# Loading v by batch and selecting the global values on chip in a two-layer attention kernel

## The chip, the cores and the metric

The kernel runs on one core of a Trainium2 chip. The metric is the device time of a run in microseconds (us). A profile of one execution gives the span from the first to the last instruction, which is a little shorter than the device time. The core has a matrix engine (TensorE, PE in the profile; its weight loads are PEld), VectorE (DVE), ScalarE (ACT), GpSimd (POOL), and SyncE (SP), which only issues transfers (DMA) here. Each engine works through its own instructions in order and waits for others by semaphores.

## The reference

Two layers are computed for 4 batches of 768 positions. The first is an attention with 8 heads of 64, in which a query sees the first 8 keys ("global") and the 96 keys up to itself ("local"), with a bias that falls with the distance. Its output is the input of the second, a mixture of 4 causal attention experts of width 64, of which each position takes its best two.

```python
# layer 1: q, k, v are [4, 8, 768, 64]
scores = q @ k.T / 8
is_global = pos_k < 8
is_local  = (0 <= pos_q - pos_k) & (pos_q - pos_k < 96)
dist  = where(is_global & ~is_local, 96, abs(pos_q - pos_k))
scores = where(is_global | is_local, scores - slope[h] * dist, -1e9)
x = softmax(scores) @ v            # -> [4, 768, 512]
# layer 2
logits = x @ w_gate                # weights w of the best two of 4 experts
for e in range(4):
    ye = softmax(causal((x @ wq[e]) @ (x @ wk[e]).T / 8)) @ (x @ wv[e]) @ wo[e]
    out += w[e] * ye               # where e is among the two
# ... cut
```

## The kernel before

The work is cut into 24 units u of 128 positions, six per batch. For each unit there are stages: loads of k, q and v (`lk`, `lq`, `lv`), casts to 16 bits on GpSimd (`kc`, `qc`, `vc`), transposes of k and q (`tk`, `tq`), local scores in two halves (`sa`, `sb`) with their exponentials on ScalarE, global scores (`gs`, one for three units), global and local values (`vg`, `va`, `vb`), the transpose of the result (`tx`), and then the second layer (`pk`, `pq`, `pv` projections, `ro` routing, `ca` to `cc` causal scores, `ma` mask, `za`, `zb` values, `tz` transpose, `ou` output). A fixed string ORDER lists all stages one after the other, and each engine executes its instructions in that order.

```python
dma = nc.sync.dma_start            # SyncE's queue; S_ is ScalarE, V VectorE, G GpSimd
# NT = 6 units per batch, NH = 3, HG = 4, KB = 64, W = 159, WP = 320, VW = 65
# ... constants, on VectorE, before everything else: cut
for hh in range(2):
    r = slice(hh * KB, hh * KB + KB)
    for p in range(NP):                                   # L81: 8 instructions
        V.scalar_tensor_tensor(biasT[r, p, :], rel[r, :], -slopes[2 * p + hh] / sc1,
                               lt[r, :], op0=Alu.mult, op1=Alu.add)
# ... cut
psS = fast.enter_context(tc.tile_pool(name="psS", bufs=2, space=PSUM))   # score buffers
# ... cut
def load_v(i):                     # i counts 4 per group of 3 units: v comes by half batch
    g, hq = divmod(i, HG)
    b, r0 = divmod(g * NH, NT)
    issue = S_.dma_start if g == 0 else dma
    if hq == 0:
        fs["v", g] = raw.tile([P, HG, 2 * NH, Dh], F32, name="vf", bufs=3)
        if r0 == 0:
            for p in range(NP):                           # L232: the 8 global rows of v
                issue(vgbuf[b % 2][32 * p:32 * p + 2 * NG, 0:Dh],
                      v[b, 2 * p:2 * p + 2, 0:NG, :])
    for hf in range(2):                                   # L235: 64 partitions, 96 KB
        issue(fs["v", g][hf * KB:(hf + 1) * KB, hq, :, :],
              v[b, hf * HG + hq, r0 * P:(r0 + NH) * P, :].rearrange("(c j) d -> j c d", j=KB))

def cast(u, nm):
    if nm != "v":
        # ... cut: q and k, L243, G.tensor_copy to 16 bits
        return
    v16, first = take("vbuf", u)
    if first:
        G.memset(v16[:, :, :, Dh:VW], 1.0)                # L247: a column of ones
    r = u % NH                                            # L249
    G.tensor_copy(v16[:, :, :, 0:Dh], fs["v", u // NH][:, :, 2 * r:2 * r + 2, :]
                  .rearrange("r h c d -> r c h d"))

def globals_in(b):                 # GpSimd: global keys, and global values with a mask
    # ... cut: kg
    G.tensor_tensor(vg[:, :, :], vgbuf[b % 2][:, :].unsqueeze(1).to_broadcast([P, H, VW]),
                    vmask[...], op=Alu.mult)              # L278, mask cut

def local_scores(u, g):
    if u not in as_:
        as_[u], first = take("abuf", u)
        if first:                                         # 5 buffers, zeroed on first use
            G.memset(as_[u][:, :, :, 0:KB], 0.0)          # L312
            G.memset(as_[u][:, :, :, KB + W:WP], 0.0)     # L313
    # ... cut: matmuls L319 (bias), L326 (scores); exponential L329 into abuf

def local_values(u, i):            # L356: 32 matmuls of 64x65 per unit (16 in a batch's first)
    # ... cut
    # then reciprocal of the sums (L363) and product (L365) on VectorE
```

Of the kernel before, what the change touches and what calls it, by code (L numbers as in the profile page):

```python
# [19 lines left out]
P = 128  # L20
# [3 lines left out]
def kernel(  # L24
# [23 lines left out]
    WP = KB + W + P - (W - P)  # L48
# [17 lines left out]
    with tc.tile_pool(name="setup", bufs=1) as setup:  # L66
        rel_i = setup.tile([P, W], I32)
        G.iota(rel_i[:, :], pattern=[[1, W]], channel_multiplier=-1, base=0)
        rel = setup.tile([P, W], F32)
        V.tensor_copy(rel[0:KB, :], rel_i[0:KB, :])  # L70
        V.tensor_scalar(rel[KB:P, :], rel_i[KB:P, :], float(KB), None, op0=Alu.add)
        ge = setup.tile([P, W], F32)
        V.tensor_scalar(ge[:, :], rel[:, :], 0.0, None, op0=Alu.is_ge)
        lt = setup.tile([P, W], F32)
        V.scalar_tensor_tensor(lt[:, :], rel[:, :], float(NL), ge[:, :],
                               op0=Alu.is_lt, op1=Alu.mult)
        V.tensor_scalar(lt[:, :], lt[:, :], -1.0, -NEG, op0=Alu.add, op1=Alu.mult)
        for hh in range(2):
            r = slice(hh * KB, hh * KB + KB)
            for p in range(NP):  # L80
                V.scalar_tensor_tensor(biasT[r, p, :], rel[r, :], -slopes[2 * p + hh] / sc1,  # L81
                                       lt[r, :], op0=Alu.mult, op1=Alu.add)
            V.tensor_copy(ident2[r, :], ident[r, r])


    row_i = const.tile([P, 1], I32)
    G.iota(row_i[:, :], pattern=[[0, 1]], channel_multiplier=1, base=0)
    key_i = const.tile([P, 1], I32)
    V.tensor_scalar(key_i[:, :], row_i[:, :], NG - 1, None, op0=Alu.bitwise_and)
    key_f = const.tile([P, 1], F32)  # L90
    V.tensor_copy(key_f[:, :], key_i[:, :])
    col_i = const.tile([P, P], I32)
    G.iota(col_i[:, :], pattern=[[1, P]], channel_multiplier=0, base=0)
    col_f = const.tile([P, P], F32)
    V.tensor_copy(col_f[:, :], col_i[:, :])
    grel = const.tile([P, P], F32)
    V.tensor_scalar(grel[:, :], col_f[:, :], key_f[:, :], None, op0=Alu.subtract)
    g_lo = const.tile([P, P], F32)
    V.tensor_scalar(g_lo[:, :], grel[:, :], 0.0, NEG, op0=Alu.is_ge, op1=Alu.mult)
    g_hi = const.tile([P, P], F32)  # L100
    V.tensor_scalar(g_hi[:, :], grel[:, :], float(NL), None, op0=Alu.is_lt)
    gmask = const.tile([P, P], F16)
    V.tensor_mul(gmask[:, :], g_lo[:, :], g_hi[:, :])
    gbias = const.tile([P, 1], F32)
    for p in range(NP):
        V.memset(gbias[32 * p:32 * p + 32, :], -slopes[2 * p] * NL)
    odd_i = const.tile([P, 1], I32)
    V.tensor_scalar(odd_i[:, :], row_i[:, :], NG, None, op0=Alu.bitwise_and)
    odd = const.tile([P, 1], F32)
    V.tensor_copy(odd[:, :], odd_i[:, :])  # L110
    V.tensor_scalar(odd[:, :], odd[:, :],
                    (slopes[1] / slopes[0] - 1.0) / NG, 1.0,
                    op0=Alu.mult, op1=Alu.add)
    V.tensor_mul(gbias[:, :], gbias[:, :], odd[:, :])


    vmask = const.tile([P, NP, 2], F32)
    G.memset(vmask[:, :, :], 1.0)
    G.affine_select(out=vmask[:, :, :], in_=vmask[:, :, :], pattern=[[-32, NP], [-NG, 2]],
                    channel_multiplier=1, base=0, compare_op=Alu.is_ge, fill=0.0)  # L120
    G.affine_select(out=vmask[:, :, :], in_=vmask[:, :, :], pattern=[[32, NP], [NG, 2]],
                    channel_multiplier=-1, base=NG - 1, compare_op=Alu.is_ge, fill=0.0)
    kmask = const.tile([P, 32], F16)
    V.memset(kmask[:, :], 0.0)
    V.memset(kmask[0:Dh, 0:NG], 1.0)
    V.memset(kmask[Dh:P, NG:2 * NG], 1.0)
# [62 lines left out]
    def ring(name, n, shape):  # L189
        rings[name] = [big.tile(shape, F16, name=f"{name}{i}") for i in range(n)], {}  # L190

    def take(name, u):

        bufs, owner = rings[name]
        first = u % len(bufs) not in owner
        owner[u % len(bufs)] = u
        return bufs[u % len(bufs)], first

    def held(name, u):
        bufs, owner = rings[name]  # L200
        assert owner[u % len(bufs)] == u
        return bufs[u % len(bufs)]

    ring("abuf", NA, [P, 2, HG, WP])
    ring("vbuf", NV, [P, 2, HG, VW])
    ring("v2buf", NV2, [P, E, VW])
    vgbuf = [big.tile([P, VW], F32, name=f"vgbuf{i}") for i in range(2)]
    for t in vgbuf:
        G.memset(t[:, 0:Dh], 0.0)
        G.memset(t[:, Dh:VW], 1.0)  # L210


    fs, kqT, gl, ags, xTs, kqs, lgs, wts, a2s, as_, done = ({} for _ in range(11))
    s16s, zs_, x16s, routing, zss, zts, tps, ppss, zs2 = ({} for _ in range(9))

    def load(u, nm):
        b, ri = divmod(u, NT)
        f = fs[nm, u] = raw.tile([P, H, Dh], F32, name=nm + "f")
        dma(f[:, :, :], {"k": k, "q": q}[nm][b, :, ri * P:(ri + 1) * P, :]  # L219
            .rearrange("h j d -> j h d"))  # L220

    def load_v(i):


        g, hq = divmod(i, HG)
# [592 lines left out]
```

## Time and profile before

| | |
|---|---|
| device time, three runs | 169.4, 169.53, 171.94 us; median 169.53 |
| the profiled run | 169.96 us, span 168.1 us, mean granted TensorE clock 0.978 |
| chain that ended last, by engine | PE 45%, DMA 19%, SyncE's queue 17%, POOL 4%, DVE 4% |
| transfers | 27.88 MB, mean 166 GB/s, pieces of 256 bytes nearly throughout |
| the two transfer queues' share of 16 engines | 64.5% and 2.1% |
| loads of k and q | 24 each of 256 KB |
| loads of v | 56 on SyncE's queue and 8 on ScalarE's, of 96 KB each |
| loads of the global rows of v | 12 and 4, of 4 KB each |

Busy time counts the instructions of an engine that run, with overlapping ones counted once. A wait is idle time of an engine in front of an instruction, put down to what ended it: "A <- B" reads "A waited for B". The chain that ended last is followed back from the last instruction to whatever released it, step by step. "L356" is line 356 of the kernel. In the timeline a row gives the start, the length, the engine, the line, the operation, output <- input and the count of instructions, and in brackets the idle time before it with what ended it.

### The profile page before, as it was taken

The page shows a single profiled execution, that of the slowest core. Times are in us where ns is not written, and L with a number is a line of the kernel's source. Part 1 is how long each engine was busy: PE and PEld are TensorE (multiplying, and loading weights), DVE is VectorE, ACT ScalarE, POOL GpSimd, SP SyncE. Part 2 cuts the span into 40 slices and gives each one's busy share as a digit, 9 for nine tenths or more (in the row PEclk, how much of TensorE's full clock was granted, in tenths as well). Part 3 has the DMA queues.
Part 4 walks back from the last instruction along what each step waited for, and adds up shares of the span by engine and source line. Part 5 has one row for each costly group of instructions (what it writes and reads, how often), then busy time and mean ns, then how long its engine had stood idle before and what let it go on. Part 6 is the DMA issues. An engine that isn't in the chain of part 4 may idle for free.

```text
span 168.1 us, 6984 instructions
## 1 busy us (share of the span) xinstructions
PE 135.2 (80%) x2918; PEld 104.1 (62%) x2918; DVE 108.2 (64%) x338; ACT 91.7 (55%) x137; POOL 90.7 (54%) x246
## 2 busy tenths in 40 slices
PE   0446499979999779959999789929999999999710
PEld 0234277958867559738778569717776788776400
DVE  7631246468887748747877578715787786887520
ACT  0007227472966537755756764516769867589420
POOL 4550999994956086618666496158632253533100
PEclk9999999999999999999999999996999999999995
DMA  5999975994897697479985837896246112031550
GB/s 127 258 273 287 241 141 131 228 210 107 187 207 169 157 274 176 99 165 293 243 196 116 221 90 180 212 233 159 96 115 188 66 66 102 28 131 64 193 194 12
DMA packets 86296, 27.88 MB, mean 166 GB/s; under 512 B 82928, under 2 KB 82928, under 8 KB 86256
## 3 DMA queue, kind: packets, MB, share of 16 engines
q1 hardware_dynamic: 82984, 26.54, 64.5%
q10 hardware_dynamic: 3272, 0.80, 2.1%
q8 instruction: 25, 0.41, 1.0%
q14 instruction: 15, 0.12, 0.2%
HBM read 21.05 MB, written 6.29 MB: 163 GB/s over the span
## 4 chain that ended last, share of the span: by engine, by line
PE 45%; DMA 19%; SPq 17%; POOL 4%; DVE 4%; issue 3%; ACT 3%; POOLq 0%; ACTq 0%; DVEq 0%
PE pps L386 8%; SPq L235 8%; DMA vf<-in_v_dram 8%; DMA qf<-in_q_dram 6%; PE cps L434 5%; PE zps L356 5%; PE vps L400 5%; PE zps L462 4%; SPq L219 4%; PE ops L490 4%; SPq L232 4%; PE tp L257 4%; PE sps L319 3%; DMA kf<-in_k_dram 3%; PE xps L371 2%
## 5 line engine op out<-in xcount | busy, mean ns | idle before, releaser
L437 ACT ACTIVATE a<-cps 128x1024 f16<-128x1024 f32 (+1 forms) x48 | 42.2, 917 | 16.2 <-PE cps L434 16.0
L329 ACT ACTIVATE abuf<-sps 128x636 f16<-128x636 f32 (+1 forms) x48 | 30.8, 683 | 24.3 <-PE sps L326 24.0
L249 POOL CAST vbuf<-vf 128x512 f16<-128x512 f32 x24 | 14.4, 616 | 25.9 <-DMA vf<-in_v_dram 19.7
L356 PE MATMUL zps<-vbuf,abuf 64*128 64x65 f16 x704 | 15.9, 193 | 10.7 <-POOL vbuf L249 9.3
L266 DVE COPY kqT<-tp 128x1024 f16<-128x1024 f16 x24 | 16.4, 690 | 9.4 <-PE tp L257 9.2
L356 PEld LDWEIGHTS <-abuf 64*128 64x128 f16 x704 | 14.6, 96 | 12.6 <-issue 10.5
L449 POOL TENSOR_SCALAR_AFFINE_SELECT a<-a 128x256 f16<-128x256 f16 x48 | 18.3, 409 | 5.7 <-ACT a L437 5.4
L391 DVE CAST kq<-pps 128x512 f16<-128x512 f32 x24 | 16.5, 690 | 6.2 <-PE pps L386 5.9
L243 POOL CAST s16q<-qf 128x512 f16<-128x512 f32 x24 | 14.7, 613 | 10.5 <-DMA qf<-in_q_dram 10.4
L363 DVE RECIPROCAL rinv<-zps 128x8 f32<-128x8 f32 x24 | 5.0, 206 | 20.1 <-PE zps L356 20.0
L493 ACT ACTIVATE osb<-ops 128x512 f32<-128x512 f32 x24 | 14.1, 598 | 6.6 <-PE ops L490 2.1
L365 DVE TENSOR_TENSOR x<-zps,rinv 128x512 f16<-128x512 f32 x24 | 16.6, 691 | 0.8
L257 PE MATMUL tp<-ident,s16k 128*128 128x128 f16 x96 | 10.8, 243 | 7.4 <-POOL s16k L243 7.4
L243 POOL CAST s16k<-kf 128x512 f16<-128x512 f32 x24 | 14.8, 617 | 3.0 <-DMA kf<-in_k_dram 2.4
L319 PE MATMUL sps<-biasT,ident 64*64 64x318 f16 (+1 forms) x192 | 15.1, 319 | 0.9 <-ACT ag L300 0.9
L462 PE MATMUL zps<-v2buf,a 128*128 128x65 f16 x336 | 15.3, 194 | 0.2
L386 PE MATMUL pps<-xT,wq 128*128 128x128 f16 x192 | 14.6, 219 | 0.0
L386 PE MATMUL pps<-xT,wk 128*128 128x128 f16 x192 | 14.6, 219 | 0.0
L326 PE MATMUL sps<-kqT 64*64 64x159 f16 (+2 forms) x384 | 14.5, 232 | 0.0
L490 PE MATMUL ops<-wo,zt 128*128 128x512 f16 x48 | 14.1, 390 | 0.4 <-DVE zt L483 0.4
L400 PE MATMUL vps<-wvg,xT 128*128 128x260 f16 x96 | 14.1, 275 | 0.1
L462 PEld LDWEIGHTS <-a 128*128 128x128 f16 x336 | 13.2, 98 | 1.5 <-DVE zs L473 0.6
(98 smaller groups left out, 257.2 us busy)
## 6 DMA issues: line engine op xcount, KB each, us to landing
kf<-in_k_dram SPq DMA_DIRECT2D x24, 256.0 KB, 3.8
qf<-in_q_dram SPq DMA_DIRECT2D x24, 256.0 KB, 4.9
out_dram<-osb SPq DMA_DIRECT2D x24, 256.0 KB, 2.8
vf<-in_v_dram SPq DMA_DIRECT2D x56, 96.0 KB, 3.0
vf<-in_v_dram ACTq DMA_DIRECT2D x8, 96.0 KB, 4.3
w<-in_moe_wk_dram SPq DMA_DIRECT2D x1, 512.0 KB
w<-in_moe_wq_dram SPq DMA_DIRECT2D x1, 512.0 KB
w<-in_moe_wv_dram SPq DMA_DIRECT2D x1, 512.0 KB, 4.5
```

Source lines behind the costliest of these rows:

```text
L243: G.tensor_copy(s16s[nm, u][:, :, :], f[:, :, :])
L257: nc.tensor.transpose(tps[u][:, i, p, :], s16s["kq"[i], u][:, 2 * p:2 * p + 2, :].rearrange("j h d -> j (h d)"), ident[:, :])
L319: mm(s_ps[o, hh, 0:2 * w].rearrange("r (c n) -> r c n", c=2), lhsT=ident2[r, :], rhs=biasT[r, p, 0:w].unsqueeze(1).to_broadcast([KB, 2, w] ...
L329: S_.activation(as_[u][:, :, 2 * g:2 * g + 2, KB:KB + w], s_ps[:, :, 0:2 * w].rearrange("r h (c n) -> r h c n", c=2), func=Exp, scale=sc1)
L356: mm(zs_[u][:, hf, hq * VW:(hq + 1) * VW], lhsT=held("abuf", u - prev)[r, hq % 2, hq // 2 * 2 + c, at:at + P], rhs=held("vbuf", u - prev)[ ...
L365: V.tensor_tensor(x16s[u][:, :, :, :], z4[:, :, :, 0:Dh], rinv.unsqueeze(3).to_broadcast([P, 2, HG, Dh]), op=Alu.mult)
L386: mm(p_ps[:, i, ep, :], lhsT=w[:, ko, ep, :, :].rearrange("r a d -> r (a d)"), rhs=xT[:, ko, :], start=(i == 0 and ep == 0 and ko == 0), s ...
L400: mm(v_ps[:, :], lhsT=xT[:, ko, :], rhs=wvg16[:, ko, :], start=(ko == 0), stop=(ko == NK - 1))
L437: S_.activation(a2[:, :, 4 * c:4 * c + len(part), :], s_ps[:, :, 0:len(part), :], func=Exp, scale=sc2)
L449: G.affine_select(out=d, in_=d, pattern=[[0, NEP], [1, P]], channel_multiplier=-1, base=0, compare_op=Alu.is_ge, fill=0.0)
L462: mm(z_ps[:, e, :], lhsT=a2[:, e % 2, (e // 2) * n + ci, :], rhs=held("v2buf", b * NT + ci)[:, e, :], start=(e == 0 and ci == 0), stop=Tru ...
L490: mm(o_ps[:, :], lhsT=zts[u][:, ep, :], rhs=wo16[:, ep, :], start=(ep == 0), stop=(ep == NEP - 1))
```

## The change

The change has four parts and a new ORDER. (1) v is loaded per head for a whole batch (192 KB an issue; the first batch still in two halves), and the separate small loads of the global rows go away. (2) The global values, which stand in rows 0 to 7 of the v already on chip, are brought to the partitions that the global values' matmul needs by a matmul with a selection matrix of zeros and ones, and copied from PSUM by ScalarE; the masked product on GpSimd goes. (3) The first three k loads are issued by ScalarE, so that two queues issue at the start; the weights wk come first on SyncE's queue; ScalarE loads its table early and casts the first two q. (4) The constants are built in the order in which they are needed, the bias in 4 instructions over 128 partitions in place of 8 over 64; the zeros of the score buffers are written by VectorE, in a new layout with smaller gaps, and the columns of ones by one instruction per ring of buffers. ORDER is new throughout: the stages are the same, with `vs` (selection), `xb`, `xg` (constants), `az` (zeros) and `xt` (table) added. It is for fewer issues on SyncE's queue, less work on GpSimd, and an earlier start.

```diff
+        V.tensor_scalar(rel[up, :], rel[up, :], slopes[1] / slopes[0], None, op0=Alu.mult)
+        for p in range(NP):
+            V.scalar_tensor_tensor(biasT[:, p, :], rel[:, :], -slopes[2 * p] / sc1, lt[:, :],
+                                   op0=Alu.mult, op1=Alu.add)
+        for r in (slice(0, KB), up):
             V.tensor_copy(ident2[r, :], ident[r, r])
# ... cut
+        V.memset(sel[:, :, :], 0.0)
+        for hq in range(HG):
+            at = hq // 2 * 32 + hq % 2 * NG
+            V.tensor_copy(sel[:, hq, at:at + NG], ident2[:, 0:NG])
# ... cut
+    abufs = [big.tile([P, 2, 2, WA], F16, name=f"abuf{i}") for i in range(NA)]
+
+    def local_zeros(i):
+        V.memset(abufs[i][:, :, :, W:2 * P], 0.0)
+        V.memset(abufs[i][:, :, :, 2 * P + W:WA - KB], 0.0)
+
+    ring("vbuf", NV, [2, HG, VW], Dh)
+    ring("v2buf", NV2, [E, VW], Hd)
# ... cut
         f = fs[nm, u] = raw.tile([P, H, Dh], F32, name=nm + "f")
-        dma(f[:, :, :], {"k": k, "q": q}[nm][b, :, ri * P:(ri + 1) * P, :]
-            .rearrange("h j d -> j h d"))
+        issue = S_.dma_start if nm == "k" and u < 3 else dma
+        issue(f[:, :, :], {"k": k, "q": q}[nm][b, :, ri * P:(ri + 1) * P, :]
+              .rearrange("h j d -> j h d"))
# ... cut
-        g, hq = divmod(i, HG)
-        b, r0 = divmod(g * NH, NT)
-        issue = S_.dma_start if g == 0 else dma
-        if hq == 0:
-            fs["v", g] = raw.tile([P, HG, 2 * NH, Dh], F32, name="vf", bufs=3)
-            if r0 == 0:
-                for p in range(NP):
-                    issue(vgbuf[b % 2][32 * p:32 * p + 2 * NG, 0:Dh],
-                          v[b, 2 * p:2 * p + 2, 0:NG, :])
+
+        b, hq = divmod(i - HG, HG) if i >= 2 * HG else (0, i % HG)
+        c0, c1 = ((0, NT), (NT, 2 * NT))[i // HG] if i < 2 * HG else (0, 2 * NT)
+        if hq == 0 and c0 == 0:
+            fs["v", b] = raw.tile([P, HG, 2 * NT, Dh], F32, name="vf", bufs=2)
         for hf in range(2):
-            issue(fs["v", g][hf * KB:(hf + 1) * KB, hq, :, :],
-                  v[b, hf * HG + hq, r0 * P:(r0 + NH) * P, :]
-                  .rearrange("(c j) d -> j c d", j=KB))
+            (S_.dma_start if i < HG else dma)(
+                fs["v", b][hf * KB:(hf + 1) * KB, hq, c0:c1, :],
+                v[b, hf * HG + hq, c0 * KB:c1 * KB, :].rearrange("(c j) d -> j c d", j=KB))
+
+    def act_tables(_):
+        S_.activation(warm[:, :], warm[:, :], func=Exp)
 
     def cast(u, nm):
-        if nm != "v":
-            f = fs[nm, u]
-            s16s[nm, u] = pp.tile([P, H, Dh], F16, name="s16" + nm)
-            G.tensor_copy(s16s[nm, u][:, :, :], f[:, :, :])
-            return
-        v16, first = take("vbuf", u)
-        if first:
-            G.memset(v16[:, :, :, Dh:VW], 1.0)
-        r = u % NH
-        G.tensor_copy(v16[:, :, :, 0:Dh], fs["v", u // NH][:, :, 2 * r:2 * r + 2, :]
-                      .rearrange("r h c d -> r c h d"))
+        s16s[nm, u] = pp.tile([P, H, Dh], F16, name="s16" + nm)
+        if nm == "q" and u < 2:
+            S_.copy(s16s[nm, u][:, :, :], fs[nm, u][:, :, :])
+        else:
+            G.tensor_copy(s16s[nm, u][:, :, :], fs[nm, u][:, :, :])
+
+    def cast_v(u):
+        b, ri = divmod(u, NT)
+        G.tensor_copy(take("vbuf", u)[:, :, :, 0:Dh],
+                      fs["v", b][:, :, 2 * ri:2 * ri + 2, :].rearrange("r h c d -> r c h d"))
# ... cut
-        vg = pp.tile([P, H, VW], F16, name="vg", bufs=2)
-        G.tensor_tensor(vg[:, :, :],
-                        vgbuf[b % 2][:, :].unsqueeze(1).to_broadcast([P, H, VW]),
-                        vmask[:, :, :].rearrange("r a b -> r (a b)").unsqueeze(2)
-                        .to_broadcast([P, H, VW]), op=Alu.mult)
-        gl[b] = (kg, vg)
+
+    def select_values(b):
+
+        g_ps = psS.tile([P, 2, 4 * P], F32, name="vgps", tag="s")
+        vgs[b] = pp.tile([P, HG, VW], F16, name="vg", bufs=2)
+        for hq in range(HG):
+            for hf in range(2):
+                r = slice(hf * KB, hf * KB + KB)
+                mm(g_ps[r, hf, hq * VW:(hq + 1) * VW], lhsT=sel[r, hq, :],
+                   rhs=held("vbuf", b * NT)[r, 0, hq, :], start=True, stop=True,
+                   skip_group_check=True, tile_position=(r.start, r.start))
+        for hf in range(2):
+            r = slice(hf * KB, hf * KB + KB)
+            S_.copy(vgs[b][r, :, :].rearrange("r h d -> r (h d)"), g_ps[r, hf, 0:HG * VW])
# ... cut
-            as_[u], first = take("abuf", u)
-            if first:
-                G.memset(as_[u][:, :, :, 0:KB], 0.0)
-                G.memset(as_[u][:, :, :, KB + W:WP], 0.0)
+            as_[u] = abufs[u % NA]
# ... cut
-lk0 kc0 tk0 lk1 lk2 kc1 lq0 lq1 lk3 lv0 qc0 lq2 qc1 lv1 qc2 tk1 tq0 kc2 lv2 gi0 lv3 vc0 vc1 tq1
-kc3 tk2 tq2 gs0 sa0 lk4 lk5 lq3 sa1 qc3 sb0 lq4 vg0 va0 vb0 sb1 tx0 tk3 tq3 vg1 lq5 va1 vb1 kc4
-qc4 wi0 vc2 kc5 qc5 tk4 sa2 vg2 wi1 sb2 tk5 wc0 lv4 wc1 tq4 lv5 tq5 va2 vb2 sa3 sb3 lv6 tx1 gs1
# ... cut
+az0 wi0 lk0 lq0 lq1 xt0 lk1 lk2 kc0 tk0 kc1 kc2 lk3 xb0 wc0 tk1 qc0 lq2 kc3 xg0 qc1 qc2 tq0 gi0
+lq3 qc3 lv0 tq1 tk2 lv1 lv2 lv3 tq2 lk4 vc0 sa0 sb0 tk3 lq4 lq5 az1 gs0 vc1 tq3 kc4 az2 sa1 lk5
+az3 wi1 wi2 qc4 az4 vc2 vs0 sa2 vg0 va0 vb0 tk4 tq4 lv4 lv5 qc5 lv6 sb1 sb2 tx0 kc5 wc1 wc2 lk6
+kc6 vg1 lv7 va1 vb1 sa3 lq6 sb3 tk5 tq5 lk7 tx1 vc3 vg2 lk8 va2 vb2 vc4 gs1 pk0 pq0 tx2 sa4 sb4
+pk1 pq1 lq7 qc6 lk9 lq8 lq9 vg3 ca0 pv0 pv1 ca1 pv2 va3 vb3 lv8 ma0 kc7 pk2 pq2 tk6 vc5 tq6 sa5
+sb5 lv9 qc7 kc8 kc9 tx3 lv10 lv11 vg4 qc8 va4 vb4 ca2 tk7 tq7 pk3 pq3 sa6 lq10 ro0 pv3 tx4 ro0
# ... cut
```

## The prediction

> **What bounds the kernel now.** I read the page's busy shares and slices first, then the list of waits, then the timeline of the stretches in which TensorE stands still. Busy shares and slices (each digit is a slice of 4.2 us, in tenths):
>
> ```profile
> PE 135.2 (80%) x2918; PEld 104.1 (62%) x2918; DVE 108.2 (64%) x338; ACT 91.7 (55%) x137; POOL 90.7 (54%) x246
> ...
> PE   0446499979999779959999789929999999999710
> ...
> PEclk9999999999999999999999999996999999999995
> DMA  5999975994897697479985837896246112031550
> ```
>
> TensorE (PE) is the busiest engine, and everything else feeds it. Its row shows three kinds of loss: a start of about 20 us (slices 1 to 5), dips in the middle (7, 7, 5, 7, 2), and an end of two slices. By windows, PE is busy 7.6 us of the first 20 us, 127.4 of the 140 us from 20 to 160, and 0.24 of the last 8. So of 168.1 us, 12.4 + 12.6 + 7.8 us are PE idle. The last 7.8 us are the last output transfers and a final check of the sums; the change leaves both as they are, and the last twelve stages of the order are the same. What can be won lies in the first two parts. Who makes PE wait, from the list of waits (total, times, longest):
>
> ```profile
> POOL vbuf L249 <- DMA vf<-in_v_dram: 19.7, 5, 5.5
> ...
> PE zps L356 <- POOL vbuf L249: 9.3, 6, 3.4
> ```
>
> The local value matmuls (L356) wait for the cast of v on GpSimd (POOL), and that waits for the v transfer. In the timeline of PE these are four dips after the start; the bracket is the idle time before the row:
>
> ```profile
> 60.00 0.66 PE L356 MATMUL zps<-vbuf,abuf 64*128 64x65 f16 x32 [2.13 <-POOL vbuf L249]
> 75.69 0.42 PE L356 MATMUL zps<-vbuf,abuf 64*128 64x65 f16 x16 [2.01 <-POOL vbuf L249]
> 95.48 0.66 PE L356 MATMUL zps<-vbuf,abuf 64*128 64x65 f16 x32 [0.90 <-POOL vbuf L249]
> 112.60 0.42 PE L356 MATMUL zps<-vbuf,abuf 64*128 64x65 f16 x16 [3.43 <-POOL vbuf L249]
> ```
>
> With one of 0.23 us at 49 us they sum to 8.7 us. Why is v late? The timeline of SyncE's own queue (SPq) shows DMA issues back to back from 0.79 to 126.6 us, and the issues by source line give their length (min/median/max in ns):
>
> ```profile
> L235 SPq DMA_DIRECT2D vf<-in_v_dram x56: 602/624/2136, 17.4 to 125.7; - x56
> L219 SPq DMA_DIRECT2D kf<-in_k_dram x24: 372/748/2120, 0.8 to 111.4; - x24
> L232 SPq DMA_DIRECT2D vgbuf<-in_v_dram x12: 612/633/2515, 36.7 to 97.1; - x12
> ```
>
> A k or q issue of 256 KB can be done in 0.37 us. A v issue of 96 KB never takes less than 0.60, and a vgbuf issue of 4 KB takes the same 0.61: it goes with the count of such issues, not with bytes. At 96 KB per 0.62 us v is issued at about 158 GB/s, while the transfers reach 293 GB/s in the best slice. In the middle v is late because one queue issues too many small loads in order; hence the 17% of SPq in the chain that ended last.
>
> The 3.43 us dip costs twice: in the stretch from 112.6 to 116.4 us the granted clock is 0.55, against 1.00 before and after. A half clock for 3.4 us is about 1.7 us of lost work.
>
> At the start the first value matmuls are held by two things. The timeline of PE:
>
> ```profile
> 17.73 0.24 PE L356 MATMUL zps<-vbuf,abuf 64*128 64x65 f16 x2 [0.62 <-POOL vbuf L249]
> 19.35 0.56 PE L356 MATMUL zps<-vbuf,abuf 64*128 64x65 f16 x14 [1.38 <-POOL abuf L312]
> ```
>
> v lands at about 17 us, then GpSimd zeroes score buffers (L312, L313) before PE may go on. GpSimd is busy 10.0 of 10 us from 20 to 30 and 9.0 from 30 to 40.
>
> [...] 56 + 12 such issues at 0.62 to 0.63 us are 42.5 us of one queue. [...] after 3.43 us idle, 0.55; after the dips of 2 us, 1.00. [...] the one load here takes 1283 ns, and at 13.5 us it stands in front of the first exponentials.
>
> **The change, part by part.**
>
> 1. v by batch. v issues on SyncE go from 56 to 32 (48 of the 64 v loads become 24 of twice the size; the first 8 stay on ScalarE's queue), the 12 vgbuf issues go away, and three k issues move to ScalarE. At 0.62, 0.63 and 0.37 us: 24 x 0.62 + 12 x 0.63 + 3 x 0.37 = 23.6 us less on a queue that is full for 126 us. The new issue carries 192 KB; if it still takes 0.62 us (estimate, from 4 KB and 96 KB costing the same), v is issued at 317 GB/s and the transfer, no longer the issue, sets the pace. Price: the first cast of a batch waits for 1.5 MB instead of 0.75, some 3 us more at 270 GB/s. In the new order that load stands well ahead: I counted the PE work that the order puts between a load and its first use, with a time for each stage from the chain (0.22 us for four transposes, 0.40 for a half of local scores, 0.48 for a unit's local values, 0.89 for q and k projections, 0.45 for v, 0.43 for an output). The loads of batches 2, 3 and 4 stand 11, 10 and 29 us of work ahead of their first value matmul; before, the six later loads stood 6, 12, 12, 18, 10 and 5 us ahead. I expect three quarters of the 8.7 us back: -6.5.
> 2. With the long dip gone its half clock goes: -1.7.
> 3. GpSimd loses zeroing (L312 5 x 0.525, L313 5 x 0.751 = 6.4), the ones (L247 1.1, L404 1.3, replaced by two memsets of some 0.2), the masked product (L278, 4 x 1.06 = 4.3) and two q casts (1.2): about 14 of 90.7 us. Zeroing moves to VectorE with only the gaps written (130 columns x 4 in place of 1288), perhaps 10 x 0.2 us. On the path of the end only the 1.38 us and a little of the crowded 20 to 40 us: -1.5.
> 4. The start. Casting q on ScalarE frees GpSimd, the table load comes early. But the 512 KB of wk now go ahead of q: at 270 GB/s that is 1.9 us. q0, cast at 7.0 us now, should come at about 8.5; ScalarE's v issues begin after it, so v lands at about 19 instead of 17 us. VectorE's constants (about 7 us either way; the bias is 4 x 0.42 where it was 8 x 0.42, but gmask, gbias and the selectors now stand ahead of the first copy) end at about 8 us in both. PE meanwhile gets one more unit of scores done. So: later by 1, ahead by 1: 0, give or take 2.
> 5. Selection matmul. 4 x 8 matmuls of 64x65, at L356's rate (32 in 0.48 us [...]) 0.25 to 0.45 us a batch: +1.5 [...]. Two ScalarE copies of 64x260 per batch, about 0.35 us each from the 128x384 activation's 0.58, 2.8 us on an engine 55% busy. For the first two batches only one to two groups of PE work stand between selection and use, so a wait of about 0.5 us each: +1.0.
>
> Sum: -6.5 - 1.7 - 1.5 + 0 + 1.5 + 1.0 = -7.2 us. The whole order of stages is new as well, and I give it no term of its own. 168.1 - 7.2 = 160.9 of span; the profiled run's time is 1.9 above its span, the median 1.4 above, so about **162.0 us**, 4.4% less.
>
> **Rivals.**
> - The transfers become the bound. For: the DMA row has many slices at 9 up to 120 us, and queues 1 and 10 fill 66.6% of the span. Against: that is 0.666 x 168.1 = 112 us of transfer work in all, and the slices between hold 4s and 5s. If v bursts delay k and q instead, the waits change their name (casts of q and k already wait 10.4 and 2.4 us) and the time is 166 to 169.
> - The start gets worse: wk ahead of q, v behind two q casts. If v lands at 21 us, all moves by 2 to 3 us: 164 to 165.
> - Selection makes a round trip PE, ScalarE, PE in score buffers of which there are two. If it costs 1.5 us a batch, 166; it would show as L353 waiting for L297.
> - The new order is simply denser. By the count of step 1, with the waits above taken out, PE needs about 1.2 us for 1 us of counted work between 20 and 50 us, and 1.05 after 120. If an unloaded GpSimd and early loads remove that, 155 to 157.
>
> **Range and chances.** The first three rivals reach up to 167, the last down to 155; a mixed outcome is likelier than any alone. Range 155.5 to 167.5. Over 2% faster means under 166.1: the term of v alone nearly reaches it, hence 0.82; within 2% 0.13; slower 0.05.
>
> **What would show it.** Right: SyncE's queue has gaps or ends its loads well before 126 us; 192 KB issues near 0.62 us; no PE dip on the v cast over 1 us; granted clock 1.00 after the start. Step 3: no memset between the first casts of v. Step 4: first kqT copy between 8.5 and 10.5 us, first reciprocal near 20. Step 5: 32 short matmuls and eight ScalarE copies of about 0.35 us. Wrong: 192 KB issues at 1.2 us, dips on k or q casts instead, or a start beyond 22 us.

## The result and the profile after

The changed kernel takes 163.09 us in the median of four runs (161.29 to 165.37), against 169.81 us of the kernel before, run beside it. The ratio is 0.951, interval 0.946 to 0.956; it leaves out runs that were disturbed. The profiled run took 161.48 us with a span of 159.8 us, against 168.1 us of span before. Later the same kernel was measured once more, on another chip of the same kind: 162.89 us (160.1 to 164.42), ratio 0.967, interval 0.956 to 0.978. So the gain is some 3 to 5% (2 to 5% by the intervals), and a difference of one per cent between two kernels below is not read as a difference.

The busy shares and slices of the changed kernel's page (one slice is now 4.0 us):

```profile
PE 134.5 (84%) x2950; PEld 105.3 (66%) x2950; DVE 111.1 (70%) x350; ACT 96.7 (61%) x148; POOL 78.8 (49%) x203
...
PE   0246599998968999987999999999999999999710
...
PEclk9999999999995999999999999999999999999985
DMA  4999994899899989899899976532210101126350
```

PE's row has two dips left in the middle (6 and 7) where it had five. The row of transfers stands, but for one slice, at 8 or 9 until about 92 us and then falls away: SyncE's last load is issued at 98 us, where it was 126. GpSimd lost 11.9 us of work. The clock row still has a 5.

From the list of waits:

```profile
PE vgps L292 <- POOL vbuf L256: 5.3, 3, 2.0
```

From the pages' groups of instructions, before and after, the casts of v (busy time and mean ns of one, then the idle time of GpSimd in front of them and what ended most of it):

```profile
L249 POOL CAST vbuf<-vf 128x512 f16<-128x512 f32 x24 | 14.4, 616 | 25.9 <-DMA vf<-in_v_dram 19.7
```

```profile
L256 POOL CAST vbuf<-vf 128x512 f16<-128x512 f32 x24 | 14.3, 620 | 16.4 <-DMA vf<-in_v_dram 9.3
```

GpSimd's idle time in front of the casts of v fell from 25.9 to 16.4 us. The share put down to v, 19.7 and 9.3, is not the whole of it: the profile puts the waits before the casts of batches 2 and 3 (2.72 and 4.37 us) down to a load of k and the load of wo, but in the built program these casts wait for their eight loads of v alone. TensorE's wait for the cast fell from 9.3 to 5.3 us and changed its place. It stands no longer at the local values but at the selection (L292), which is now the first reader of a batch's v. In PE's timeline, the bracket being the idle time before the row:

```profile
19.63 0.27 PE L292 MATMUL vgps<-vbuf,sel 64*64 64x65 f16 x3 [1.82 <-POOL vbuf L256]
48.57 0.43 PE L292 MATMUL vgps<-vbuf,sel 64*64 64x65 f16 x8 [2.01 <-POOL vbuf L256]
72.77 0.32 PE L292 MATMUL vgps<-vbuf,sel 64*64 64x65 f16 x8 [1.47 <-POOL vbuf L256]
```

After the start that is 2.01 + 1.47 = 3.5 us, against 8.7. TensorE's waits at the turns (transposes) of k and q, which the larger loads of v might have lengthened, stayed as they were: 7.4 + 2.2 us before, 7.0 + 2.4 after. The issues, with min/median/max in ns and first and last start in us:

```profile
L240 SPq DMA_DIRECT2D vf<-in_v_dram x32: 595/656/2128, 21.2 to 89.9; - x32
...
L228 SPq DMA_DIRECT2D kf<-in_k_dram x21: 368/982/2602, 4.0 to 97.0; - x21
...
L228 SPq DMA_DIRECT2D qf<-in_q_dram x24: 368/874/2043, 1.3 to 98.2; - x24
```

The first line has 8 issues of 96 KB in it; the 24 of 192 KB alone took 596 ns at the shortest and 659 in the median, so an issue of twice the size still takes about 0.6 us. But the medians of k and q rose from 0.75 and 0.62 us to 0.98 and 0.87 with the same shapes, the shortest still at 0.37: these issues now seem to wait. The profile names nothing that they wait for; with the transfers' row at 8 or 9, my estimate is that it is room among the transfers, and no run shows it.

The span can be cut at the first and at the last normalization on VectorE (one of the first layer, one of the second). By windows, the middle part before and after, with its length and PE's busy time:

```profile
19.96:157.66 137.70, 125.80 (x2822) 98.80 (x2823) 97.80 (x290) 86.12 (x129) 80.77 (x216) 0.99 0.64 158
```

```profile
21.76:150.02 128.26, 123.33 (x2826) 98.88 (x2826) 97.06 (x289) 88.18 (x134) 68.90 (x177) 0.99 0.66 165
```

The start is 1.8 us longer, but PE does 1.8 us more work in it (9.32 us busy in place of 7.52). The middle is 9.4 us shorter. Of that 7.0 is idle time of PE (11.90 to 4.93 us), 1.8 is the work moved into the start, and 0.7 is shorter busy time. The end is 0.7 shorter. 1.8 - 9.4 - 0.7 = -8.3 us, which is the whole difference of the spans.

### The profile page after: what moved, and what is told of

Read it like the earlier page. It is cut to its first block, busy times and chain, and to the rows that moved or that the text cites. A ratio compares the mean times of both kernels' runs of the same rounds, so it can differ in the third digit from the quotient of the medians.

```text
span 159.8 us, 6967 instructions
## 1 busy us (share of the span) xinstructions
PE 134.5 (84%) x2950; PEld 105.3 (66%) x2950; DVE 111.1 (70%) x350; ACT 96.7 (61%) x148; POOL 78.8 (49%) x203
## 3 DMA queue, kind: packets, MB, share of 16 engines
q1 hardware_dynamic: 79264, 25.71, 64.8%
HBM read 20.98 MB, written 6.29 MB: 171 GB/s over the span
## 4 chain that ended last, share of the span: by engine, by line
PE 55%; DMA 17%; SPq 13%; POOL 4%; issue 3%; DVE 2%; ACT 1%; ACTq 0%; POOLq 0%; DVEq 0%
PE pps L398 10%; SPq L240 9%; PE zps L471 6%; PE cps L443 6%; DMA kf<-in_k_dram 5%; PE vps L412 5%; DMA vf<-in_v_dram 5%; PE ops L499 5%; PE zps L368 4%; DMA qf<-in_q_dram 4%; SPq L228 4%; PE sps L331 4%; PE tp L264 3%; PE xps L383 3%; PE sps L338 2%
## 5 line engine op out<-in xcount | busy, mean ns | idle before, releaser
L256 POOL CAST vbuf<-vf 128x512 f16<-128x512 f32 x24 | 14.3, 620 | 16.4 <-DMA vf<-in_v_dram 9.3
L264 PE MATMUL tp<-ident,s16k 128*128 128x128 f16 x96 | 10.5, 238 | 7.0 <-POOL s16k L252 7.0
L331 PE MATMUL sps<-biasT,ident 64*64 64x318 f16 (+1 forms) x192 | 15.8, 329 | 0.0
L252 POOL CAST s16q<-qf 128x512 f16<-128x512 f32 x22 | 13.5, 618 | 4.2 <-PE cps L443 1.5
L368 PE MATMUL zps<-vbuf,abuf 64*128 64x65 f16 x704 | 15.3, 192 | 0.0
L398 PE MATMUL pps<-xT,wq 128*128 128x128 f16 x192 | 15.1, 223 | 0.0
L338 PE MATMUL sps<-kqT 64*64 64x159 f16 (+2 forms) x384 | 15.0, 239 | 0.0
L443 PE MATMUL cps<-kq,kq 64*128 64x128 f16 x240 | 13.8, 222 | 0.0
```

The lines of the kernel that those rows point to most:

```text
L252: G.tensor_copy(s16s[nm, u][:, :, :], fs[nm, u][:, :, :])
L331: mm(s_ps[o, hh, 0:2 * w].rearrange("r (c n) -> r c n", c=2), lhsT=ident2[r, :], rhs=biasT[r, p, 0:w].unsqueeze(1).to_broadcast([KB, 2, w] ...
L338: mm(s_ps[o, hh, c * w:c * w + n], lhsT=kqT[b][r, 0, p, k0:k0 + KB], rhs=kqT[b][r, 1, p, k0:k0 + n], start=False, stop=True, skip_group_ch ...
L368: mm(zs_[u][:, hf, hq * VW:(hq + 1) * VW], lhsT=as_[u - prev][r, hq % 2, hq // 2, at:at + P], rhs=held("vbuf", u - prev)[r, c, hq, :], sta ...
L398: mm(p_ps[:, i, ep, :], lhsT=w[:, ko, ep, :, :].rearrange("r a d -> r (a d)"), rhs=xT[:, ko, :], start=(i == 0 and ep == 0 and ko == 0), s ...
L443: mm(s_ps[:, e2, i, :], lhsT=kqs[b * NT + ci][r, 0, ep, :], rhs=kqs[u][r, 1, ep, :], start=(i == 0), stop=True, skip_group_check=True)
```

## The experiments

Each ratio is to the kernel before, run beside it on the same chip. The first four kernels ran together, then the next four, then the last four.

**Splitting the v loads again.** The changed kernel, with each 192 KB load of v cut into two of 96 KB.

```
-        for hf in range(2):
+        for c0, c1 in ([(c0, c1)] if i < 2 * HG else [(0, NT), (NT, 2 * NT)]):
+            for hf in range(2):
```

> The changed kernel with each 192 KB load of v split again into two of 96 KB, same bytes, same place in the order; ratio to the kernel before of the changed kernel: 0.951. Theory (the number of issues on SyncE's queue held v back): 24 more issues at 0.6 us put 14 us back on the queue, the loads end some 10 us later, the waits of PE for the cast of v grow from 5.3 us to 8 or more, ratio 0.97 to 0.98. Rival (up to 95 us the transfers themselves are the bound, the queue only waits for them): the queue's time is absorbed, ratio 0.95 to 0.957.

Measured: 170.4 us, ratio 1.004, interval 1.000 to 1.007. The whole gain is gone, more than I expected. The last load is issued at 105.5 us in place of 98.2. PE's timeline and its middle part (first to last normalization):

```profile
49.05 0.43 PE L293 MATMUL vgps<-vbuf,sel 64*64 64x65 f16 x8 [2.89 <-POOL vbuf L257]
76.66 0.43 PE L293 MATMUL vgps<-vbuf,sel 64*64 64x65 f16 x8 [3.83 <-POOL vbuf L257]
```

```profile
20.70:156.28 135.58, 127.41 (x2826) 101.85 (x2826) 96.56 (x289) 88.15 (x134) 69.15 (x177) 0.95 0.63 157
```

The two waits are longer by 0.9 and 2.4 us. The idle time of the middle is 135.58 - 127.41 = 8.2 us, 3.2 more than in the changed kernel, but the busy time for the same instructions is up as well, by 4.1 us, at a mean clock of 0.95 in place of 0.99. With each of the two waits goes a half-clock stretch of 6.8 us, from 48.5 and from 75.8 us; in the changed kernel's profile there is one of 3.4 us. So what the merged loads bring is real, and in these two profiles the larger part of it is clock, not idle time. Over all the runs the mean granted clock is 0.951 with v split (20 runs) and 0.969 in the changed kernel (8 runs).

**The merged loads alone.** The kernel before in its own order, with v of batches 2, 3 and 4 in 192 KB loads; everything else stays, the 4 KB loads of the global rows too.

```
-        fs["v", g] = raw.tile([P, HG, 2 * NH, Dh], F32, name="vf", bufs=3)
+        # once a batch
+        fs["v", b] = raw.tile([P, HG, 2 * NT, Dh], F32, name="vf", bufs=2)
...
+        if b and r0:
+            return
+        c0, c1 = (0, 2 * NT) if b else (2 * r0, 2 * r0 + 2 * NH)
```

> The kernel before with its old order, and v of batches 2 to 4 loaded whole, in 192 KB issues, at the place of the first half's loads; the small loads of the global rows stay. Theory (issue count): 24 fewer issues free 15 us of SyncE's queue, at least half of the 8.7 us of PE waits for v go, ratio 0.97 to 0.98. Rival (only the new order puts v early enough; merging alone delays k and q behind the larger bursts): the waits move to the casts of k and q, ratio 0.99 to 1.01.

Measured: 164.6 us, ratio 0.975, interval 0.965 to 0.985. Half of the gain or more, by the least of the changes. Where four waits of the local values stood before, two are left, and only one is long:

```profile
51.14 0.62 PE L358 MATMUL zps<-vbuf,abuf 64*128 64x65 f16 x16 [2.12 <-POOL vbuf L251]
...
106.77 0.42 PE L358 MATMUL zps<-vbuf,abuf 64*128 64x65 f16 x16 [0.64 <-POOL vbuf L251]
```

**wk behind the first q loads.** The changed kernel, with the load of wk third in place of first.

```
-az0 wi0 lk0 lq0 lq1 xt0 ...
+az0 lk0 lq0 lq1 wi0 xt0 ...
```

> The changed kernel with the wk load moved behind the first two q loads on SyncE's queue. Theory (wk ahead of q costs the start): first cast of k at about 4 us and first reciprocal about 20 us instead of 5.9 and 21.8, and the end moves with it, ratio 0.940 to 0.945. Rival (from 20 to 80 us PE waits for transfers whose total is unchanged, so an earlier start is only waited away at the selection of the next batch): the first reciprocal comes earlier, the selection of the second batch still starts at about 48.6 us, ratio 0.949 to 0.953.

Measured: 160.95 us, ratio 0.951, interval 0.940 to 0.962. The first normalization comes at 20.98 us in place of 21.76; the unchanged kernel, run again further down, has it at 22.54, so this much lies within what two runs of one kernel differ by. The selections of batches 2 and 3 come at nearly the same moment as in the changed kernel, after a shorter wait:

```profile
48.93 0.31 PE L292 MATMUL vgps<-vbuf,sel 64*64 64x65 f16 x8 [1.08 <-POOL vbuf L256]
71.71 0.31 PE L292 MATMUL vgps<-vbuf,sel 64*64 64x65 f16 x8 [0.94 <-POOL vbuf L256]
```

Beside the changed kernel's own 0.951 and 0.967 this is the lowest median of a complete kernel in this study, but no gain that can be told from theirs. What the selections wait less, the turns of k and q wait more (8.3 + 3.4 us in all, against 7.0 + 2.4): the rival's account, with another place for the wait.

**Only one batch of v.** The changed kernel with v loaded for the first batch alone: 24 loads and 4.7 MB are left out, and the later batches use the first one's v, so this computes something else; its time is a floor.

```
+        if i >= 2 * HG:
+            return
+        b, hq = 0, i % HG
...
-                      fs["v", b][:, :, 2 * ri:2 * ri + 2, :]...
+                      fs["v", 0][:, :, 2 * ri:2 * ri + 2, :]...
```

> The changed kernel with v of the first batch alone loaded and used for all four batches: leaves out 24 issues and 4.7 MB, all other work the same. Theory (what PE still waits for between 20 and 80 us is v, its issues and its bytes): the waits of the selection for v (2.0 and 1.5 us) go, and with them the waits for k and q behind v, ratio 0.92 to 0.93. Rival (PE is full and the dips are incidental): ratio 0.945 to 0.95.

Measured: 156.07 us, ratio 0.919, interval 0.910 to 0.928. The waits for v at the second and third selection are gone, the clock of the middle is 1.00, and PE is nearly full in it:

```profile
22.64:145.92 123.28, 121.21 (x2826) 97.44 (x2826) 96.42 (x289) 87.85 (x134) 68.38 (x177) 1.00 0.51 132
```

Idle time in the middle is 2.1 us. So another 3 to 5% hangs on v's transfers and what they hold up; below that PE's work itself is the bound.

**The changed kernel again**, unchanged, as the measure for those run with it.

> The changed kernel unchanged, on the chip of the next three, as their yardstick. Ratio 0.946 to 0.956.

Measured: 162.89 us, ratio 0.967, interval 0.956 to 0.978, waits of 1.59 and 1.04 us at the second and third selection. The first cast of v comes at 19.75 us and the first normalization at 22.54, each 0.8 us later than in the first profile.

**The old order.** The changed code with the stages in the order of before, the new stages put in where their results are needed.

```
-ORDER = the changed kernel's
+ORDER = that of before, + xt0, xb0, xg0, az0 to az4, vs0 to vs3; lv of batches 2 to 4: every second group
```

> The code of the changed kernel with the order of the kernel before: loads of v by batch at the first half's place, constants and the table load first, the zeros of a score buffer ahead of its first use, the selection ahead of its batch's first global values, wk at its old place. Theory (merging v is most of the gain, with GpSimd's relief): better than merging alone in the old order (0.975), 0.955 to 0.97. Rival (the new order is worth as much as the merging): 0.975 to 0.99.

Measured: 162.85 us, ratio 0.964, interval 0.955 to 0.972, the same as with the new order. But the waits are others. In PE's timeline:

```profile
49.82 0.27 PE L353 MATMUL zps<-vg,ag 64*128 64x260 f16 x1 [0.52 <-ACT vg L297]
73.84 0.66 PE L353 MATMUL zps<-vg,ag 64*128 64x260 f16 x2 [1.19 <-ACT vg L297]
106.62 0.66 PE L353 MATMUL zps<-vg,ag 64*128 64x260 f16 x2 [0.70 <-ACT vg L297]
```

Here the selection's round trip over ScalarE is bare: with 0.46 us in the first batch it comes to 2.9 us. The new order hides it (0.1 us in all before L353) and pays instead with the waits for v at the selections of batches 2 and 3, which here have none.

**The masked product back.** The changed kernel with the global values as before: sixteen loads of 4 KB, and a masked product on GpSimd in place of the selection.

```
+            for p in range(NP):
+                (S_.dma_start if i < HG else dma)(
+                    vgbuf[b % 2][32 * p:32 * p + 2 * NG, 0:Dh], v[b, 2 * p:2 * p + 2, 0:NG, :])
...
-        for hq in range(HG): ... selection matmuls and ScalarE copies
+        G.tensor_tensor(vgs[b], vgbuf[b % 2] (broadcast), vmask (broadcast), op=Alu.mult)
```

> The changed kernel with the global values made the old way: 16 loads of 4 KB, 12 of them on SyncE's queue, and the masked product on GpSimd (4 x 1.06 us) in place of the selection matmuls. Theory (each issue of 0.61 us on a full queue delays the loads behind it): 2.4 us more of queue ahead of each batch's v, the first value work of batches 2 and 3 later by as much, ratio 0.96 to 0.97. Rival (the selection's own wait for v on PE is worth as much as the small loads): 0.945 to 0.955.

Measured: 180.27 us, ratio 1.061, interval 1.047 to 1.076: far off both expectations, and slower than the kernel before, which does the same product. Two kernels further down take it apart.

**v in two loads a batch.** The changed kernel with v of batches 2 to 4 in loads of 768 KB.

```
+        if i >= 2 * HG:
+            for hf in range(2 if hq == 0 else 0):
+                dma(fs["v", b][hf * KB:(hf + 1) * KB, :, :, :].rearrange("r h c d -> r (h c) d"),
+                    v[b, hf * HG:(hf + 1) * HG, :, :].rearrange("h (c j) d -> j (h c) d", j=KB))
+            return
```

> The changed kernel with v of batches 2 to 4 in two issues of 768 KB each instead of eight of 192 KB, all at the place of the first. Theory (an issue costs about 0.6 us whatever it carries): 18 fewer issues, up to 11 us less queue time; v of a batch stands complete earlier, the selection's waits of 2.0 and 1.5 us shrink, ratio 0.935 to 0.945. Rival (192 KB per 0.65 us is already faster than the transfers move, so the queue only waits for them): same ratio as the changed kernel within 0.005.

Measured: 166.07 us, ratio 0.973, interval 0.957 to 0.989; no better than the changed kernel's 0.967. The profile is of the longest of its four runs (166.73 us). The line of v's issues, and the wait that came for it:

```profile
L241 SPq DMA_DIRECT2D vf<-in_v_dram x6: 827/2624/5592, 37.3 to 81.1; - x6
```

```profile
75.10 0.61 PE L269 MATMUL tp<-ident,s16k 128*128 128x128 f16 x4 [4.22 <-POOL s16k L257]
```

An issue of 768 KB takes 0.83 us at its shortest and 2.6 in the median; the 1.8 us between them I take for waiting. k behind it comes late, and TensorE now waits 4.2 us at a turn of k. Fewer issues than with 192 KB brought nothing here. All of a batch's v also moved to the place of its first load, so size and place are not told apart.

**The small loads alone.** The changed kernel with its selection, and the sixteen 4 KB loads added, into buffers that nothing reads.

```
+    vgbuf = [big.tile([P, VW], F32, name=f"vgbuf{i}") for i in range(2)]
...
+            for p in range(NP):
+                (S_.dma_start if i < HG else dma)(
+                    vgbuf[b % 2][32 * p:32 * p + 2 * NG, 0:Dh], v[b, 2 * p:2 * p + 2, 0:NG, :])
```

> The changed kernel with the selection kept, and the sixteen 4 KB loads of the global values put back in, four ahead of each batch's v, landing in buffers that nothing reads. It asks what made the kernel with the masked product so slow (1.061). If the loads did it (they hold the ScalarE queue at the start and slow the transfers beside them), this kernel is slow too: ratio 1.01 to 1.06, with first v cast and first reciprocal stage 2 to 5 us later and fewer GB/s in the first 30 us. If the product and its place in GpSimd's order did it, this kernel is within the sixteen issues x 0.64 us, part of them hidden: 0.97 to 0.99.

Measured: 178.59 us, ratio 1.056, interval 1.042 to 1.071. The first cast of v comes at 27.24 us and the first normalization at 30.04, each 8.3 us later than in the changed kernel, where the first story had 2 to 5. ScalarE issues v only after the four small loads, which take it 3.2 us.

**The product alone.** As the masked product, but without the sixteen loads: the product is of constants, so the global values are not those of the input.

```
-        for hq in range(HG): ... selection matmuls and ScalarE copies
+        G.tensor_tensor(vgs[b], vgbuf[b % 2] (constants), vmask (broadcast), op=Alu.mult)
```

> The changed kernel with the masked product on GpSimd in place of the selection, but of a constant: the sixteen 4 KB loads are left out (so the global values are not those of the input). The other half of the same question. If the loads did the harm, this kernel stands at 0.96 to 0.975, as the changed kernel: four products of 1.06 us on GpSimd, less 32 short matmuls and eight ScalarE copies. If the product's place in GpSimd's order did it, TensorE still waits 2 to 7 us for it in each batch: 1.01 to 1.05.

Measured: 173.82 us, ratio 1.029, interval 1.018 to 1.040, and TensorE waits for the product, as the second story said: 5.74, 7.47 and 0.57 us in three of the batches.

```profile
60.18 0.40 PE L357 MATMUL zps<-vg,ag 64*128 64x260 f16 x2 [7.47 <-POOL vg L298]
```

The product stands behind casts and a mask in GpSimd's order: in batch 2 it ends 3.4 us after the casts of v that the order puts before it. But those casts themselves begin at 55.53 us, where it was 47.90 in the changed kernel, and the first of all at 23.09 for 18.96. So neither story holds alone: both halves are slow, and v is late in both. What they share is seen in the page's line of SyncE's transfers (packets, MB, and the time that they took as a share of 16 engines' span). The changed kernel run again (span 158.4 us), the product alone (172.3 us), the small loads alone (176.8 us):

```profile
q1 hardware_dynamic: 79264, 25.71, 65.4%
```

```profile
q1 hardware_dynamic: 79264, 25.71, 70.7%
```

```profile
q1 hardware_dynamic: 79480, 25.75, 69.1%
```

The first two move the same packets and bytes. They take 0.654 x 158.4 = 103.6 us of 16 engines in one and 0.707 x 172.3 = 121.8 us in the other, 18% more. It is so from the beginning, where both load the same tiles in the same order. The rate by slice of the changed kernel run again, and of the product alone:

```profile
GB/s 109 288 284 277 271 195 128 157 255 221 205 227 231 229 247 219 229 259 250 203 285 203 216 229 170 119 132 113 94 66 4 70 4 70 68 72 221 180 209 12
```

```profile
GB/s 117 226 218 209 208 219 150 177 202 206 196 175 186 216 227 207 198 179 213 191 200 255 182 186 233 205 126 126 61 65 65 4 65 61 67 65 214 167 183 4
```

For the longer packet time, the cause that fits, an estimate of mine, is one that I put in without seeing it. The two new buffers of 260 bytes a partition stand ahead of the load tiles in memory and push them. In the built programs the tiles of k, q and v begin at a multiple of 512 bytes in the kernel before, in the changed kernel and in its variants without the new buffers, and at 64 (small loads) or 96 bytes (both kernels with the product) past one in these three. With the 256-byte pieces of these loads the packet time, worked out as above, is 103 to 105 us in the changed kernel, with wk late, with v split, with the old order, and in the two kernels below, which ran beside two of the three (107.8 with v in two loads); and 122 to 123 us in these three. Per packet the kernel before costs the same as the changed one (108.4 us for 82984, 103.6 for 79264). A run that shifts the address and nothing else was not made, so this is a fit over three kernels against the others, not shown, and how much of the 13.9 us between the two spans it explains, beside the waits for the product, is open. What follows surely: these three kernels cannot price the masked product or the small loads against the changed kernel. Against each other the two halves differ by 2.7% with intervals that don't overlap, so where transfers are slow, sixteen small loads cost more than the product in place of the selection.

**Zeros by GpSimd.** The changed kernel with the score buffers' zeros written by GpSimd again.

```
-        V.memset(abufs[i][:, :, :, W:2 * P], 0.0)
-        V.memset(abufs[i][:, :, :, 2 * P + W:WA - KB], 0.0)
+        G.memset(abufs[i][:, :, :, W:2 * P], 0.0)
+        G.memset(abufs[i][:, :, :, 2 * P + W:WA - KB], 0.0)
```

> The changed kernel with the zeros of the score buffers written by GpSimd again, not VectorE. Theory (the prediction's third step: GpSimd relief is worth 1.5 us, the zeros a good half of it): ten memsets before the first v casts on GpSimd, some 2.5 to 4 us, put the first v cast and the first reciprocal stage about 1 us later: ratio 0.970 to 0.978 if the changed kernel stands at 0.9672. Rival: GpSimd waits for v's transfer at that point anyway (its v cast waited 5.5 us for the load), so the memsets lie in that wait: nothing, 0.960 to 0.972.

Measured: 163.23 us, ratio 0.963, interval 0.952 to 0.975: no cost that can be told. The reason of the rival is not what the trace shows. The memsets stand not in the wait for v but between its first casts, which puts the second cast at 21.60 us. The first cast comes at 20.53 us and the first normalization at 23.33, against 18.96 and 21.76 in one run of the changed kernel and 19.75 and 22.54 in the other, so against the later of the two 0.8 us is left. In the new layout they add only 2.1 us to GpSimd's busy time (80.9 for 78.8).

**v first in the queue.** wk late, and in batches 2 and 3 v loaded ahead of one k and one q tile, whose casts and turns stand later.

```
-... lv8 lv9 lv10 lv11 behind lk9 lq9; tk9 tq9 ahead of vs1
+... lk9 lq9 behind lv11; kc9 qc9 behind vc7; tk9 tq9 behind vb6
(the same for lk16 lq16, lv15, vc12, vb12; wi0 behind lq1)
```

> A candidate: the changed kernel with wk loaded after the first two q tiles, and in batches 2 and 3 v loaded ahead of one k and one q tile, whose casts and turns move behind the selection. Theory: what is left to gain is the wait for v at the selection (1.6 and 1.0 us, with the half clock after the longer one); v lands about 2 us earlier, both waits go: 0.940 to 0.950, against 0.9505 with wk late alone. Rival: the queue is bound by transfers there, so the wait moves to the k and q tile that were put behind, as it did with v in two issues: 0.950 to 0.965, TensorE waits at the turn of that tile.

Measured: 162.58 us, ratio 0.961, interval 0.948 to 0.974. The wait at the selection is gone: the second batch's starts at 46.58 us with no idle time before it. What came in its place, in PE's timeline and in windows of 2 us (length, PE's busy time, and the clock as the third figure from the end):

```profile
49.17 0.40 PE L264 MATMUL tp<-ident,s16q 128*128 128x128 f16 x4 [0.47 <-POOL s16q L252]
...
50.35 0.46 PE L338 MATMUL sps<-kqT 64*64 64x159 f16 x8 [0.52 <-DVE kqT L273]
```

```profile
48.00:50.00 2.00, 1.32 (x27) 0.72 (x20) 1.47 (x4) 0.00 (x0) 1.58 (x4) 1.00 0.95 216
50.00:52.00 2.00, 1.33 (x24) 0.94 (x23) 0.37 (x2) 1.08 (x2) 1.53 (x3) 0.60 1.16 263
52.00:54.00 2.00, 2.00 (x32) 1.54 (x29) 0.71 (x2) 1.45 (x2) 1.41 (x4) 0.54 1.00 227
```

The tile of q that was put behind is waited for now, in several short pieces, and the half clock comes all the same. The time agrees with the rival (0.950 to 0.965), and so does the place of the wait: around 50 us the order of the queue chose who waits, and won nothing that can be told.

## Why the prediction was right, and which of its steps were not

The time came out at 163.09 us for a predicted 162.0, the span at 159.8 for 160.9. The sum held better than its terms, and that is in part luck: the terms below miss in both directions. The last step of the sum is wrong as well: 160.9 with 1.4 or 1.9 on top is 162.3 or 162.8, not 162.0.

- **Step 1, v by batch (-6.5).** Right in mechanism, near in size. The 192 KB issue kept its 0.6 us, the queue ended its loads 28 us sooner, and PE's waits on v after the start fell by 8.7 - 3.5 = 5.2 us. Splitting the loads gives the whole gain back, and merging them alone in the old order gives about half of it, so this step carries the change. What I got wrong in it is the sign "no dip over 1 us": 2.01 and 1.47 us are left. I had counted 11 and 10 us of work between a load and its first value matmul. The first of these was there: TensorE came to the selection of batch 2, which stands a little ahead of that matmul, at 46.56 us, 10.2 us after the first of the eight v issues (36.34). What was too small is the time that 1.5 MB take: the eight issues filled the queue for 7.2 us and the cast began at 47.90, 11.6 us after the first of them. The first rival, transfers becoming the bound, thus came true in part: issues of k and q lengthened (in the median by 0.23 and 0.25 us), and both attempts to go on past it (v in two loads, v first) only moved the wait.
- **Step 2, the half clock gone (-1.7).** Wrong. The dip of 3.43 us is gone, but a half-clock stretch of the same length now follows the one of 2.01 us. By windows of the changed kernel:

```profile
46.50:48.60 2.10, 0.09 (x4) 0.12 (x4) 0.49 (x2) 0.19 (x1) 0.70 (x2) 0.99 0.80 181
48.60:52.00 3.40, 3.40 (x62) 2.76 (x61) 1.20 (x3) 1.57 (x4) 3.40 (x7) 0.50 1.09 248
```

  So the sentence "after the dips of 2 us, 1.00" was true of two dips of one run and no rule. Over all the runs the mean clock is 0.967 for the kernel before (37 runs) and 0.969 for the changed one (8 runs), so no gain in clock is shown; a part of the 1.7 us is not excluded. In the traces the granted clock changes in steps: in all 14 profiles every stretch of one granted clock, from the first record at 22 to 37 us to the drop at the end, lasts a whole number of 3.41 us (26, 1 and 14 of them in the kernel before, 7, 1 and 30 in the changed one). And they show what went with half clock. Cut into such windows, those at full clock in which PE was busy less than 0.49 of the time were followed by half clock in 25 cases of 25, those between 0.49 and 0.68 in 3 of 17, those above in none of 484; in the profiles of the two main kernels alone it is 4 of 4, none of 4 and none of 69. The window with the gap of 2.01 us was busy 0.41 of it, the one of the long dip before 0.09, and those of the two 2 us dips of the kernel before 0.50 and 0.51, with no half clock after them. With v first, a window busy 0.67 of it, with no wait over 0.52 us, was followed by half clock. That the length of one unbroken gap decides, which this step assumed, is thus not shown.
- **Step 3, GpSimd relief (-1.5).** The work went about as counted (11.9 us in place of 14), and no memset stands between the first casts of v. What that is worth is not shown. Giving the zeros back costs nothing that can be measured, but in the new layout they are 2.1 of the 11.9 us; the share of the product could not be priced.
- **Step 4, the start (0, give or take 2).** Right, and by its own reason: v is cast at 18.96 us (predicted 19), q0 already at 7.56 (8.5), the first copy of turned keys comes at 8.87 us (8.5 to 10.5), the first normalization at 21.76, which is later than the 20 I wrote, and the 1.8 us are paid back by 1.8 us of work done sooner. What wk ahead of q costs is not shown: without it the first normalization comes at 20.98 us, and two runs of the changed kernel itself have it at 21.76 and 22.54.
- **Step 5, selection (+1.5 and +1.0).** The matmuls are as estimated: 32 of them busy PE for 1.5 us (0.43 for the first batch's eight, 0.32 for the third's), the eight copies take 0.37 us each. The +1.0 for the round trip did not come in the new order (0.1 us); it comes in the old order, as 2.9 us. Another price, that the selection brings the need for v forward, is argued from the order and not measured: the kernel with the masked product, which could have shown it, is slow for other reasons too.
- **The order without a term.** Fair: with the old order the time is the same within what can be measured. The new one trades the round trip for waits on v at the selection.

In sum: -5.2 on v and -1.8 on other idle time stand where I had -6.5, -1.5 and +1.0; the clock gave about 0 for -1.7, and the end, for which I had nothing, 0.7. That PE's busy time includes 1.5 us of new matmuls and still fell in total by 0.7 us I can't split further.

## What to carry to other kernels

When one queue issues loads back to back and an issue takes the same time for 4, 96 or 192 KB (here 0.61, 0.60 and 0.60 us at the shortest), make the loads larger until the issues begin to wait; here the step past that, to 768 KB, brought nothing and made another tile late. Look for what becomes the first reader of the larger load, since the wait can move to it (here the selection, 2.01 and 1.47 us). Count the half clock that may follow a wait (here 0.50 for 3.4 us), and judge it by how busy TensorE was over a whole window of 3.41 us (here it always followed below 0.49), not by the longest gap. Before believing an experiment that adds a buffer, compare the packet time of the loads that it did not touch (here 103.6 and 121.8 us).

## What the runs showed of the hardware that was not expected

- 79264 packets of the same 25.71 MB took 103.6 us of 16 engines in one kernel and 121.8 us in another. It goes, in a fit that no run has tested alone, with load tiles that begin 64 or 96 bytes past a multiple of 512, in three kernels of three. In both main kernels the weight tiles begin at 192 and the output tiles at 320 past such a multiple; whether moving them pays was not tried.
- The granted clock changed in steps of 3.41 us, and a window at full clock in which PE was busy less than 0.49 of the time was followed by half clock in 25 cases of 25, whatever its longest gap; one followed a window with no single wait over 0.52 us. With v split, at a mean clock of 0.95 in place of 0.99 in the middle part, busy time added more (4.1 us) than idle time (3.2 us).
- An issue of 768 KB took 0.83 us at its shortest, where one of 192 KB took 0.60 and one of 4 KB 0.61; in the median it took 2.6 us.
